# Softmax reciprocals as powers on GpSimd, two products of zeros at the start, and a new instruction order, in a kernel of two attention blocks

## Chip, cores, metric

One core of one Trainium2 chip. The metric is the device time of one launch in microseconds, the median of several runs; lower is better. A run is called slow when it is over 1.5% above the fastest of its kernel; verdicts use the other runs, called fast.

## The reference

Two independent attention blocks over x of 2048 x 640, 32 heads of width 20, in bf16. The outputs are laid side by side. Condensed, with masks, heads and shapes as in the reference:

```python
# block A: sliding window of 256
scores = jnp.einsum("bhqd,bhkd->bhqk", q, k) * (Dh ** -0.5)
mask = (idx[:, None] - idx[None, :] >= 0) & (idx[:, None] - idx[None, :] < 256)
p = softmax(jnp.where(mask, scores, -1e9)); a = (p @ v) @ wo
# block B: linear attention, phi(t) = where(t > 0, t + 1, exp(t)) + 1e-6
num = phi(q) @ (phi(k).T @ v); den = phi(q) @ phi(k).sum(0) + 1e-6
b = (num / den) @ wo
```

## The kernel before

The kernel builds a graph of small operations and then emits them in one list, ORDER, that a search outside the kernel wrote. An entry names an operation and the engine that does it: P is TensorE (PE), A ScalarE (ACT), D VectorE (DVE), G GpSimd (POOL), S SyncE (SP). SP only issues transfers; GpSimd issues many of them too. **Each engine works through its entries in exactly that order.** An entry that isn't ready holds back everything behind it on its engine.

The end of one of 16 groups of block A (a group is four heads and half of the 2048 rows): the value products leave numerators and denominators in PSUM. They are copied to ON, of which there are two. Four of ON's rows are the denominators. One transfer (den1) gathers them in RC, in a compact shape of 128 x 32, where they are inverted into RD. A second one (den2) writes the reciprocals to DRAM, and a third (den3, in four parts) spreads them over the rows of RB, of which there is one. Only then can DVE multiply the numerators by them (norm).

```python
def evac(e, rg=rg):
    copy(e, ON[nb][:, rg * NX : (rg + 1) * NX], FB[box[rg]][:])
# ... nb alternates between 0 and 1 from group to group
dma(QS, lambda q: q.dma_start(out=RC[nb][:], in_=ON[nb][Dh : Dh + 97 : 32, :]), ...)           # den1
pl.op({"DVE": 0.34}, lambda e: nc.vector.reciprocal(out=RD[nb][:], in_=RC[nb][:]), ...)         # recip
dma(QS, lambda q: q.dma_start(out=DR[nb][:]..., in_=RD[nb][:]), ...)                            # den2
for j in range(4):                                                                              # den3
    dma(QS, lambda q, j=j: q.dma_start(out=RB[32 * j : 32 * j + 32, :], in_=DR[nb][j : j + 1, :].to_broadcast([32, TQ])), ...)
pl.op({"DVE": 1.22}, lambda e: nc.vector.tensor_tensor(out=dst, in0=ON[nb][:], in1=RB[:], op=ALU.mult), ...)  # norm
```

The number in a `pl.op` is what the search takes for the operation's duration. At the start, PE runs seven products of zeros, then turns four blocks of x by products with a unit matrix, and then makes V as soon as WV is there.

```python
for _ in range(7):
    nc.tensor.matmul(FB[0], lhsT=E1[0][:, 0:P], rhs=E1[0][:, 0:NX], start=True, stop=True)
```

The softmax here doesn't subtract the row's maximum and nothing guards it: scores larger than these inputs give would overflow.

## Time and profile before

| | before |
|---|---|
| median time, us | 265.92 (3 runs), 267.27 with the run made beside the changed kernel |
| span of the profiled run, us | 263.8 |
| busy: PE / ACT / DVE / GpSimd, us | 247.4 / 210.1 / 171.4 / 68.6 |
| PE at half clock after the start, us | 6.8 in two stretches |

The prediction below shows the lines and reads them.

### The profile page before, as it was taken

To read this page: it belongs to the slowest core of one execution; us is meant where nothing else is said; L and a number is where in the kernel's file an instruction comes from. 1 tells how busy PE (TensorE), PEld (TensorE's weight loads), DVE (VectorE), ACT (ScalarE), POOL (GpSimd) and SP (SyncE) were. 2 spreads that over 40 slices of the span, in tenths; PEclk is the share of its full clock that TensorE was granted. 3 is DMA by queue.
4 is the path that set the end of the run, shared out by engine and by line. 5 is a ranking of instruction groups with operands and counts; after the bars stand their busy time and mean duration, and the time that the engine had idled before them with its cause. 6 is when DMAs were issued, how large, how long until landed. Compare 5 with 4: busy or idle time off the path is not lost.

```text
span 263.8 us, 10316 instructions
## 1 busy us (share of the span) xinstructions
PE 247.4 (94%) x4407; PEld 146.0 (55%) x4439; DVE 171.4 (65%) x388; ACT 210.1 (80%) x236; POOL 68.6 (26%) x156
## 2 busy tenths in 40 slices
PE   6899999999879999999999999987898999999994
PEld 2555555565545545545666666544555555577772
DVE  1226476698958675755362634988999978775542
ACT  3648789899987998888868887999999999964213
POOL 8001010334411114242202156001313313264410
PEclk9799999999979999999999999999999999999999
DMA  7998953968938524394887968776688245253635
GB/s 202 257 114 208 235 119 115 148 160 120 178 102 148 140 68 126 70 180 93 246 177 184 323 195 150 132 211 138 153 194 231 57 133 190 98 165 111 236 134 197
DMA packets 68495, 42.46 MB, mean 161 GB/s; under 512 B 54858, under 2 KB 63306, under 8 KB 68438
## 3 DMA queue, kind: packets, MB, share of 16 engines
q1 hardware_dynamic: 61266, 32.48, 53.1%
q0 software_dynamic: 4560, 9.00, 13.5%
q8 instruction: 34, 0.56, 0.9%
q10 hardware_dynamic: 2624, 0.33, 0.8%
q14 instruction: 11, 0.09, 0.1%
HBM read 24.29 MB, written 10.59 MB: 132 GB/s over the span
## 4 chain that ended last, share of the span: by engine, by line
PE 74%; ACT 13%; issue 5%; DVE 5%; DMA 2%; SPq 0%; ACTq 0%
PE F L437 16%; PE F L470 9%; PE F L714 9%; PE F L758 9%; ACT PT L548 8%; PE U L542 8%; PE F L750 6%; PE F L648 6%; PE U L714 5%; PE F L835 3%; ACT E L741 3%; DMA WV<-in_A_wqkv_dram 2%; DVE R L743 1%; DVE ON L352 1%; DVE PT L577 1%
## 5 line engine op out<-in xcount | busy, mean ns | idle before, releaser
L548 ACT ACTIVATE PT<-U 128x2048 bf16<-128x2048 f32 x78 | 146.7, 1881 | 15.5 <-PE U L542 14.2
L577 DVE TENSOR_TENSOR PT<-PT,MK 128x512 bf16<-128x512 bf16 (+2 forms) x116 | 46.8, 426 | 18.1 <-ACT PT L548 18.1
L542 PE MATMUL U<-QK 20*64 20x128 bf16 (+4 forms) x1600 | 33.1, 252 | 3.3 <-ACT PT L548 2.9
L542 PEld LDWEIGHTS <-QK 20*64 20x64 bf16 x1600 | 15.4, 104 | 26.1 <-issue 24.7
L686 POOL DMA_DIRECT2D RB<-dr x35 | 17.7, 508 | 43.5 <-DMA dr<-RD 16.9
L750 PE MATMUL F<-W,X 128*128 128x320 bf16 x160 | 26.8, 303 | 1.8 <-DVE R L743 1.8
L741 ACT ACTIVATE E<-F 128x320 bf16<-128x320 f32 (+1 forms) x52 | 25.6, 502 | 3.5 <-PE F L750 3.1
L743 DVE SCALAR_TENSOR_TENSOR R<-F,E 128x320 bf16<-128x320 f32 (+1 forms) x47 | 25.9, 553 | 1.2
L458 POOL DMA_DIRECT2D dqk<-QK x29 | 15.3, 532 | 43.4 <-ACT WK L348 17.9
L835 PE MATMUL F<-X,WQ 128*128 128x512 bf16 x85 | 25.2, 383 | 1.1 <-issue 0.7
L758 PE MATMUL F<-R,XT 128*128 128x320 bf16 x160 | 25.9, 300 | 0.0
L470 PE MATMUL F<-WV,X 128*128 128x320 bf16 x120 | 23.1, 318 | 1.3 <-DMA WV<-in_A_wqkv_dram 1.3
L648 PEld LDWEIGHTS <-V 64*32 64x32 bf16 x1556 | 19.1, 93 | 8.6 <-issue 7.2
L648 PE MATMUL F<-PT,V 64*32 64x320 bf16 (+4 forms) x1452 | 23.6, 250 | 0.1
L352 DVE CAST QK<-F 128x512 bf16<-128x512 f32 x20 | 13.6, 690 | 13.8 <-PE F L437 13.7
L750 PEld LDWEIGHTS <-X 128*128 128x128 bf16 x160 | 15.1, 98 | 10.5 <-issue 3.5
L437 PE MATMUL F<-X,WK 128*128 128x512 bf16 x71 | 20.5, 380 | 0.3
L682 POOL DMA_DIRECT2D RC<-ON x11 | 8.1, 735 | 45.2 <-DVE E L742 15.5
L437 PE MATMUL F<-X,WQ 128*128 128x512 bf16 x67 | 19.4, 380 | 0.4
L352 DVE COPY ON<-F 128x512 f32<-128x512 f32 x22 | 14.7, 687 | 6.9 <-PE F L648 6.7
L758 PEld LDWEIGHTS <-XT 128*128 128x128 bf16 x160 | 14.8, 98 | 7.5 <-issue 1.0
L742 DVE TENSOR_SCALAR E<-E 128x320 bf16<-128x320 bf16 (+1 forms) x52 | 13.4, 258 | 6.9 <-ACT E L741 6.6
(104 smaller groups left out, 329.3 us busy)
## 6 DMA issues: line engine op xcount, KB each, us to landing
RB<-dr POOLq DMA_DIRECT2D x35, 128.0 KB, 3.8
RB<-dr SPq DMA_DIRECT2D x29, 128.0 KB
QK<-dqk SPq DMA_DIRECT2D x6, 512.0 KB
XT<-in_B_x_dram SPq DMA_DIRECT2D x5, 512.0 KB
out_dram<-WK SPq DMA_DIRECT2D x9, 160.0 KB
do<-OS SPq DMA_DIRECT2D x5, 256.0 KB
out_dram<-ST SPq DMA_DIRECT2D x6, 160.0 KB
out_dram<-ST POOLq DMA_DIRECT2D x6, 160.0 KB, 2.8
```

Of the source, the lines that this page charges most:

```text
L352: nc.vector.tensor_copy(out=dst, in_=src)
L437: mms.append((mm_t(NX), xread(slot, k) + [("wqk", i, m)], lambda ps, k=k: nc.tensor.matmul(ps[:], lhsT=WQK[i][:, k, m * P : (m + 1) * P], ...
L470: mms = [(mm_t(HALF), (xread(slot, k) if slot or kb > 3 else [("xb", kb)]) + [("wv", hf)], lambda ps, k=k, hf=hf: nc.tensor.matmul(ps[:, 0 ...
L542: nc.tensor.matmul(upper.at(1)[0][64 * rho : 64 * rho + 64, j, cc : cc + w], lhsT=QK[g][32 * j : 32 * j + Dh, kc : kc + 64], rhs=QK[g][32 ...
L548: nc.scalar.activation(out=pt, in_=upper.at(1)[0][:], func=ACT.Exp, scale=scale)
L577: nc.vector.tensor_tensor(out=p, in0=p, in1=mk, op=ALU.mult)
L648: nc.tensor.matmul(FB[box[rg]][32 * j : 32 * j + 32, qc : qc + w], lhsT=V[kb % NV][64 * rho : 64 * rho + 64, HV * h : HV * h + 32], rhs=PT ...
L714: mms = [(mm_t(HALF), [lkeys(c)] if not isinstance(lkeys(c), list) else lkeys(c), lambda ps, c=c, hf=hf: nc.tensor.matmul(ps[:, 0:HALF], l ...
L741: ({"ACT": act_ps(n)}, lambda e, ps: nc.scalar.activation(out=e1, in_=ps[:, 0:n], func=ACT.Exp), [], [("e1", i)]),
L750: mms = [(mm_t(HALF), [("x", slot, k), ("w1",)], lambda ps, k=k, b=b, hf=hf: nc.tensor.matmul(ps[:, 0:HALF], lhsT=X[slot][:, k, b * P : (b ...
L758: mms = [(mm_t(HALF), [("r1", tb), ("xt", c % 2)], lambda ps, tb=tb, c=c, hf=hf: nc.tensor.matmul(ps[:, 0:HALF], lhsT=XT[:, c % 2, tb, :], ...
L835: mms = [(mm_t(NX), [("x", slot, k)] + WQK0, lambda ps, k=k, c=c: nc.tensor.matmul(ps[:], lhsT=WQB[:, k, :].rearrange("p (f c) -> p c f", ...
```

## The change

The intent: take reciprocals off DVE, which is full in the ACT-bound stretches, by using GpSimd, which is idle for three quarters of the span; keep PE's clock up at the start; and let the search place everything anew. The diff, cut to what takes effect (a tile of mask constants and its products are also added, but the set that would use them is empty, and the unit matrix gets 64 more columns for them; ORDER's 150 lines of numbers are left out):

```diff
-    tinyo = T([P, 1], "tinyo", F32)
+    minus = T([P, 32], "minus", F32)
+    nc.vector.memset(minus[:], -1.0)
...
+                o.deps[0].deps += busy      # the first products of V wait for both products of zeros
...
+    def keep_busy(tb):
...
+        o = pl.op({"PE": mm_t(NX)}, lambda e: nc.tensor.matmul(FB[box[0]], lhsT=E1[0][:, 0:P], rhs=E1[0][:], start=True, stop=True), 1.0, (), (), after=[turns[tb]], ...)
...
-        pl.op({"DVE": 0.34}, lambda e: nc.vector.reciprocal(out=RD[nb][:], in_=RC[nb][:]), key, ...)
+        pl.op({"DVE": 0.34, "POOL": 0.3}, lambda e: nc.vector.reciprocal(out=RD[nb][:], in_=RC[nb][:]) if e == "DVE" else nc.gpsimd.tensor_tensor(out=RD[nb][:], in0=RC[nb][:], in1=minus[:], op=ALU.pow), key, ...)
...
+    for tb in (0, 2):
+        keep_busy(tb)
```

With the groups numbered 0 to 15, the new order gives GpSimd the reciprocals of groups 0, 4 to 9 and 11 to 14.

## The prediction

> **What bounds the kernel now.** I read the page of the kernel before first (busy shares, the 40 slices, the chain that ended last), then the busy times by stage, then the timeline and the 3.41 us windows around the two dips of the granted clock, then the waits.
>
> ```profile
> PE 247.4 (94%) x4407; PEld 146.0 (55%) x4439; DVE 171.4 (65%) x388; ACT 210.1 (80%) x236; POOL 68.6 (26%) x156
> ...
> PEclk9799999999979999999999999999999999999999
> ...
> PE 74%; ACT 13%; issue 5%; DVE 5%; DMA 2%; SPq 0%; ACTq 0%
> ```
>
> TensorE (PE) is busy 94% of the span and carries 74% of the chain. The clock row dips twice, in slices 2 and 12. The stages show that PE is not the bound everywhere (columns: stretch, its length, busy us and instructions by engine, clock, DMA share, GB/s):
>
> ```profile
> 0.00:55.00 55.00, 51.33 (x680) 28.00 (x689) 26.97 (x70) 40.28 (x53) 10.22 (x49) 0.97 0.84 172
> 55.00:78.00 23.00, 20.55 (x412) 12.09 (x419) 18.81 (x50) 21.87 (x28) 8.62 (x16) 0.95 0.81 149
> 78.00:168.00 90.00, 89.06 (x1707) 51.66 (x1701) 53.77 (x118) 75.18 (x69) 24.25 (x44) 0.99 0.69 160
> 168.00:231.00 63.00, 57.34 (x1303) 33.52 (x1316) 55.49 (x122) 61.26 (x63) 14.43 (x26) 1.00 0.58 153
> 231.00:264.00 33.00, 29.10 (x325) 20.76 (x323) 16.33 (x32) 11.50 (x27) 11.07 (x22) 0.99 0.50 169
> ```
>
> Three stretches belong to PE: 6 to 55 us, 78 to 168 us (89.06 of 90), and 231 us to the end. Two belong to ScalarE (ACT): 55 to 78 us (21.87 of 23) and 168 to 231 us (61.26 of 63), where a 1.88 us exponential starts about every 2.5 us and ACT's other work fills the rest. In those two stretches PE has slack. What PE loses at the start is this:
>
> ```profile
> 1.26 3.10 PE L312 MATMUL F<-E 128*128 128x512 bf16 x7 [1.26 <-DVE ones L308]
> 4.19 0.44 PE L487 MATMUL U<-ID,QK 128*128 128x128 bf16 x5
> 5.30 0.73 PE L487 MATMUL U<-ID,QK 128*128 128x128 bf16 x10 [0.66 <-DMA QK<-in_A_x_dram]
> 7.36 1.06 PE L470 MATMUL F<-WV,X 128*128 128x320 bf16 x4 [1.33 <-DMA WV<-in_A_wqkv_dram]
> ...
> 4.15:7.57 3.42, 1.43 (x18) 1.05 (x17) 1.15 (x3) 1.56 (x3) 2.21 (x7) 1.00 1.15 298
> 7.57:10.98 3.41, 3.41 (x18) 2.12 (x17) 0.20 (x1) 2.15 (x5) 0.00 (x0) 0.50 1.22 242
> 72.42:75.83 3.41, 1.77 (x79) 1.38 (x56) 2.35 (x6) 3.41 (x4) 0.79 (x2) 1.00 0.63 197
> 75.83:79.25 3.42, 3.42 (x64) 1.64 (x63) 1.81 (x6) 2.46 (x4) 0.00 (x0) 0.50 0.07 16
> 171.41:174.82 3.41, 2.52 (x77) 1.46 (x85) 2.72 (x6) 3.25 (x4) 0.00 (x0) 1.00 0.91 233
> ```
>
> PE waits 0.66 us for x and 1.33 us for WV. After each stretch of 3.41 us in which PE was busy only 1.43 or 1.77 us, the next 3.41 us run at half clock. A stretch with 2.52 us busy was not followed by one.
>
> **What the Trainium skill says.** "TensorE: Matmul & The Clock Gate", section "What's actually happening": a monitor gates the PE clock to half after an idle window and frees it after a busy one; the window is 3413 ns and free-running. The trace agrees: both dips last 3.41 us at 0.50. The page gives no share of activity that counts as idle; this trace brackets it between 1.77 and 2.52 us busy of 3.41. "GPSIMD Engine Reference", section 3.1, gives 4497 ns for a 2048-column fp32 add of two tensors; its 32-column share is about 70 ns beside a fixed cost. It has nothing on a power, and no GpSimd instruction of the kernel before has two tensor inputs. The small selects there take 0.24 to 0.53 us, so I take 0.3 to 1.5 us for one power, an estimate. "SBUF — State Buffer", section "Who interferes with whom": a VectorE (DVE) instruction with two SBUF inputs and a GpSimd (POOL) instruction that reads SBUF block each other. The mask multiplications (116, mean 426 ns) are of that kind, so a power may be held for some tenths of a us. The trace before cannot show it.
>
> **The change part by part.**
>
> 1. *Powers on GpSimd.* The order gives GpSimd 11 of the 16 reciprocals. DVE loses 11 x 0.348 us (row L683) = 3.8 us. DVE also waited for the denominators to land before three of the 16, 2.5 us in all (row L683 of the waits), but none of that shows as a leading part of the chain. By itself I give this 0.2 us.
>
> 2. *Copies moved.* Counting both orders, ACT loses four Q/K copies (0.586 each), one turn of x (0.69), one weight shuffle (0.91), a G, a z and an ON copy (0.42, 0.43, 0.59), and gains one output copy (0.43): -5.0 us of 210. DVE gains the same at its own rates: 4 x 0.69 + 0.82 + 0.50 + 0.485 + 0.49 + 0.69 - 0.49 = 5.3 us, less the 3.8 us: +1.4 us of 171. So ACT room is bought with DVE room, and the reciprocals pay for most of it.
>
> 3. *Where that lands.* I summed each engine's work between the same score units in both orders, with the durations of the profile's rows (PE: 0.136 us per 320 columns, 0.216 per 512, as the chain shows). Up to score unit 12 (about 55 us): PE 43.7 before, 44.1 after. Units 12 to 20 (to 78 us): ACT 23.3 and 23.3, DVE 20.1 and 19.6. Units 20 to 52 (to 168 us): PE 80.1 and 80.3, ACT 78.5 and 75.8, but PE is the bound there, so ACT's 2.7 us are worth nothing. Units 52 to 77 (to 231 us): ACT 65.7 and 65.0, PE 49.5 and 50.3. After unit 77: PE 29.1 and 28.7. Only the last two pay: -0.6 us (0.7 scaled by 210 busy over 222 summed) in the ACT stretch, and -0.4 us of PE work pulled out of the tail into that stretch's slack. The +0.2 us in units 20 to 52 goes against them. Sum: -0.8 us.
>
> 4. *The two products of zeros.* They add 2 x 0.216 us of PE work, in time where PE waits for a DMA, so they delay nothing while the data is late. They lift the busy time of the idle window from 1.43 to about 1.9 us. That is inside the bracket of 1.77 to 2.52, so the chance that the clock holds is some 60%. If it holds, 3.41 us at half clock become full: a gain of 1.7 us, in a PE-bound stretch, so it is passed on. The window is free-running, so not every execution of the kernel before need pay it. Expected: -0.9 us.
>
> 5. *The start's DMA order.* WV's first half is now issued second instead of fourth on SP, but three blocks of x now come behind it. The first V product stands behind the second zeros, which stand behind the third turn, so it needs the same 880 KB as before (three blocks of 160 KB and 400 KB of WV). The second half of WV is issued before the other weights instead of at 7.16 us. Two value projections in a row can then run, and the fourth turn no longer divides them at half clock. I give it -0.3 us.
>
> 6. *The hole at 73 to 75 us.* PE waits 0.60 us for an exponential and 1.04 us for DVE's R, and the half clock at 75.83 follows (another 1.7 us). The new order has the same load there and shuffles the B products between units 18 and 22 differently. I take an even chance that the dip goes or a similar one stays, and a small chance of a new one elsewhere: -0.5 us.
>
> Sum: -0.2 - 0.8 - 0.9 - 0.3 - 0.5 = -2.7 us. I set +0.2 us against it for longer chains of the denominators. 265.9 - 2.5 = **263.4 us**.
>
> **The rivals.**
>
> *The clock dips anyway.* For it: 1.9 us busy is nearer 1.77, which dipped, than 2.52, and the turns now wait longer for x, since WV is ahead of it. Against: with the window placed otherwise, the first V products fall into it. It leaves the time at about 264.8 us.
>
> *GpSimd's power is slow, and the normalisations wait.* Each chain is: denominators out, power, two DMAs (3.8 us for the broadcast, section of DMA issues), then a 1.2 us product in DVE's fixed order. The new order leaves some 3 to 5 us from broadcast to product, so a power of up to about 1.5 us is hidden; of 3 us or more, up to 11 products would stall DVE by 1 to 2 us each, half of it in the ACT-bound stretch where DVE is 88% busy. It would make the time 265 to 269 us. Against it: GpSimd is idle 74% of the span.
>
> *The new order removes both dips and fits better everywhere.* The two dips (3.4 us) with the holes at 6 and 73 us (about 3 us) and the 1 us of part 3 make 7 us: 258.5 to 260 us. Against it: the work per stage hardly moves, and holes tend to come back elsewhere.
>
> **Range and chances.** The first and third rivals set the lower half, the second and a new hole the upper. 80% range: 260.4 to 266.8 us. Faster by over 2% means below 260.6 us, which asks for nearly all of the third rival: 0.12. Slower by over 2% means above 271.2 us, past even the slow-power rival: 0.03. Within 2%: 0.85.
>
> **What the profile after would show.** The clock row has no dip in the second slice, and the stretch from about 4 to 7.5 us has 1.9 us or more of PE busy. GpSimd has 11 powers of 0.3 to 1.5 us, and DVE 5 reciprocals. ACT's busy time falls by about 5 us, DVE's rises by about 1. The exponentials from unit 52 on still start every 2.5 us. The tail after the last exponential is 33 us, less 0.4. It would be wrong if DVE shows waits of some us for the broadcast denominators (RB), if the first dip stays, or if the B products make a new hole of over 1.5 us between 55 and 78 us.

## The result

| | before | changed |
|---|---|---|
| median, us | 267.27 (4 runs, 265.11 to 269.84) | 290.56 (4 runs, 288.32 to 292.56) |
| ratio of fast runs | 1 | 1.0899 (95%: 1.0754 to 1.1043) |
| span of the profiled run, us | 263.8 | 287.8 |
| busy: PE / ACT / DVE / GpSimd, us | 247.4 / 210.1 / 171.4 / 68.6 | 257.5 / 206.3 / 173.0 / 126.9 |
| PE at half clock after the start, us | 6.8 | 20.5 |

A ratio is the mean time of one kernel's fast runs over that of the kernel before in the same rounds, so it isn't quite the ratio of the medians. The change is slower by 9%. From the changed kernel's page: the busy line, the clock in 40 slices, and the group of the new GpSimd instruction (count, busy us and mean ns, then idle time before it); last, the group of the reciprocals on DVE in the kernel before.

```profile
PE 257.5 (89%) x4441; PEld 147.8 (51%) x4441; DVE 173.0 (60%) x387; ACT 206.3 (72%) x227; POOL 126.9 (44%) x163
...
PEclk9999999998999999977999997799998899999999
...
L722 POOL TENSOR_TENSOR RD<-RC,minus 128x32 f32<-128x32 f32 x11 | 60.8, 5530 | 36.7 <-DMA RC<-ON 31.7
...
L683 DVE RECIPROCAL RD<-RC 128x32 f32<-128x32 f32 x16 | 5.6, 348 | 2.6 <-DMA RC<-ON 2.5
```

**One power takes 5.5 us**, where the search had 0.3 and I had 0.3 to 1.5 (mean 5.53, median 5.46). PE's busy share fell by five points, and the clock dips in four places, none of which was there before. (PE's busy time rose although only two products were added: at half clock the same products take longer: below, ten take 2.87 us in a4 and 1.52 in a1.) The stages of the changed kernel:

```profile
0.00:55.00 55.00, 52.84 (x699) 28.61 (x700) 31.56 (x80) 39.50 (x49) 18.24 (x56) 1.00 0.79 163
55.00:78.00 23.00, 18.29 (x356) 10.77 (x355) 15.70 (x43) 18.44 (x24) 7.96 (x15) 0.93 0.74 149
78.00:168.00 90.00, 82.87 (x1488) 46.39 (x1487) 48.33 (x102) 65.99 (x59) 42.28 (x35) 0.96 0.59 146
168.00:231.00 63.00, 54.99 (x1142) 30.19 (x1144) 46.95 (x105) 50.41 (x48) 32.93 (x30) 0.92 0.63 138
```

Nothing is wrong in the first 55 us: PE even does more there than before (52.84 us against 51.33). From then on neither PE nor ACT fills its stage. In the waits (who <- what it waited for: us in total, times, longest), DVE's long stand for RB, the spread reciprocals, is new. The last line is from the kernel before, where it was 1.7 us in one place.

```profile
DVE OS L732 <- DMA RB<-dr: 18.1, 5, 7.9
...
DVE QK L732 <- DMA RB<-dr: 8.4, 2, 5.4
...
DVE QK L693 <- DMA RB<-dr: 1.7, 1, 1.7
```

And in the list of SP's own waits:

```profile
SPq L723 <- POOL RD L722: 26.8, 6, 7.0
```

SP stood 27 us at transfers that wait for a power, and loads for other stages stand behind those. The largest hole shows how it goes (timeline of the changed kernel: a line of GpSimd, two of DVE and one of PE, then the 3.41 us windows of the clock):

```profile
114.47 5.46 POOL L722 TENSOR_TENSOR RD<-RC,minus 128x32 f32<-128x32 f32 x1 [4.93 <-DMA W<-in_A_wo_dram]
...
127.29 1.23 DVE L732 TENSOR_TENSOR OS<-ON,RB 128x1024 bf16<-128x1024 f32 x1 [7.85 <-DMA RB<-dr]
...
128.63 0.69 DVE L361 CAST QK<-F 128x512 bf16<-128x512 f32 x1
...
129.37 1.49 PE L480 MATMUL F<-WV,X 128*128 128x320 bf16 x5 [6.24 <-DVE QK L361]
...
122.19:125.60 3.41, 0.94 (x6) 0.39 (x4) 0.00 (x0) 2.21 (x3) 2.04 (x4) 1.00 0.51 167
125.60:129.01 3.41, 0.00 (x0) 0.00 (x0) 1.72 (x3) 0.00 (x0) 0.00 (x0) 0.50 1.00 155
129.01:132.43 3.42, 3.06 (x34) 1.43 (x34) 1.94 (x6) 0.87 (x1) 2.55 (x1) 0.50 0.50 146
```

The power ends at 119.9 us, the reciprocals are spread by 127.3, and DVE has stood still for 7.85 us. The copy that frees PE's bank (at 128.63) is behind the product in DVE's order, so PE stands still for 6.24 us. That makes a nearly idle window, and the clock is at half for the next 6.8 us.

### The profile page after: what moved, and what is told of

It is laid out like the page before. It is cut to its first block, busy times and chain, and to the rows that moved or that the text cites. A ratio compares the mean times of both kernels' runs of the same rounds, so it can differ in the third digit from the quotient of the medians.

```text
span 287.8 us, 10335 instructions
## 1 busy us (share of the span) xinstructions
PE 257.5 (89%) x4441; PEld 147.8 (51%) x4441; DVE 173.0 (60%) x387; ACT 206.3 (72%) x227; POOL 126.9 (44%) x163
## 3 DMA queue, kind: packets, MB, share of 16 engines
q0 software_dynamic: 4416, 8.87, 11.8%
## 5 line engine op out<-in xcount | busy, mean ns | idle before, releaser
L722 POOL TENSOR_TENSOR RD<-RC,minus 128x32 f32<-128x32 f32 x11 | 60.8, 5530 | 36.7 <-DMA RC<-ON 31.7
L780 ACT ACTIVATE E<-F 128x320 bf16<-128x320 f32 (+1 forms) x52 | 25.6, 501 | 11.8 <-PE F L874 5.7
L468 POOL DMA_DIRECT2D dqk<-QK x35 | 18.4, 530 | 35.4 <-DVE QK L361 19.1
L789 PE MATMUL F<-W,X 128*128 128x320 bf16 x160 | 28.9, 311 | 3.5 <-DVE R L782 3.1
L570 PEld LDWEIGHTS <-QK 20*64 20x64 bf16 x1600 | 16.3, 105 | 27.8 <-issue 26.4
L874 PE MATMUL F<-X,WQ 128*128 128x512 bf16 x100 | 29.5, 393 | 0.0
L480 PE MATMUL F<-WV,X 128*128 128x320 bf16 x120 | 19.9, 306 | 6.2 <-DVE QK L361 6.2
L725 POOL DMA_DIRECT2D RB<-dr x27 | 13.7, 509 | 25.6 <-DVE V L361 7.7
L361 DVE CAST QK<-F 128x512 bf16<-128x512 f32 x24 | 16.3, 688 | 13.6 <-PE F L447 12.6
L753 PE MATMUL F<-WV,R 128*128 128x320 bf16 x90 | 18.0, 313 | 5.5 <-DVE XT L782 2.6
L447 PE MATMUL F<-X,WQ 128*128 128x512 bf16 x75 | 20.5, 380 | 0.0
L753 PE MATMUL F<-W,OT 128*128 128x320 bf16 x80 | 16.9, 325 | 3.8 <-DMA RB<-dr 2.3
L361 DVE CAST G<-F 128x320 bf16<-128x320 f32 (+2 forms) x21 | 10.2, 487 | 15.8 <-PE F L853 6.9
```

What stands on the lines that cost most here:

```text
L361: nc.vector.tensor_copy(out=dst, in_=src)
L447: mms.append((mm_t(NX), xread(slot, k) + [("wqk", i, m)], lambda ps, k=k: nc.tensor.matmul(ps[:], lhsT=WQK[i][:, k, m * P : (m + 1) * P], ...
L570: nc.tensor.matmul(upper.at(1)[0][64 * rho : 64 * rho + 64, j, cc : cc + w], lhsT=QK[g][32 * j : 32 * j + Dh, kc : kc + 64], rhs=QK[g][32 ...
L722: pl.op({"DVE": 0.34, "POOL": 0.3}, lambda e: nc.vector.reciprocal(out=RD[nb][:], in_=RC[nb][:]) if e == "DVE" else nc.gpsimd.tensor_tenso ...
L753: mms = [(mm_t(HALF), [lkeys(c)] if not isinstance(lkeys(c), list) else lkeys(c), lambda ps, c=c, hf=hf: nc.tensor.matmul(ps[:, 0:HALF], l ...
L780: ({"ACT": act_ps(n)}, lambda e, ps: nc.scalar.activation(out=e1, in_=ps[:, 0:n], func=ACT.Exp), [], [("e1", i)]),
```

## The experiments

**Theory, slow power:** the power's 5.5 us lengthen a chain whose slack the order had used up. **Rivals:** the new order packs worse by itself; GpSimd's queue, held for 5.5 us, starts other transfers late. In all of them, "(wrong)" marks a kernel whose result is wrong on purpose. "Measured" gives the median of all runs of a kernel, slow ones too.

| run | what it is | ratio of fast runs to before (95%) |
|---|---|---|
| changed | 11 powers | 1.090 (1.075 to 1.104) |
| a1 | all reciprocals on DVE | 0.995 (0.989 to 1.001) |
| a2 | product in place of the power (wrong) | 0.994 (0.988 to 1.000) |
| a3 | old order, 11 powers | 1.116 (1.110 to 1.123) |
| a4 | a1 without the zeros | 0.997 (0.991 to 1.003) |
| b2 | power on 8 of 32 columns (wrong) | 0.991 (0.982 to 0.999) |
| b3 | power on 16 columns (wrong) | 1.012 (1.001 to 1.023) |
| b4 | queue held, mostly not the chain (wrong) | 1.044 (1.037 to 1.052) |
| d1 | queue held, never the chain (wrong) | 0.995 (0.987 to 1.003) |
| d2 / d3 | powers in the first 5 / last 6 groups | 1.042 (1.034 to 1.049) / 1.041 (1.033 to 1.049) |
| b1 / e1 | later products, with power / product (e1 wrong) | 1.083 (1.075 to 1.091) / 1.023 (1.009 to 1.038) |
| c2 / c3 | chain's transfers on GpSimd, power / product (c3 wrong) | 1.089 (1.079 to 1.099) / 0.995 (0.987 to 1.003) |
| c1 / e2 | both moves, power / product (e2 wrong) | 1.077 (1.070 to 1.084) / 1.030 (1.009 to 1.050) |
| c4 | a1 again, five rounds | 0.995 (0.988 to 1.001) |

### a1: the same order, no power

```diff
-lambda e: nc.vector.reciprocal(...) if e == "DVE" else nc.gpsimd.tensor_tensor(..., op=ALU.pow)
+lambda e: nc.vector.reciprocal(...)
```

> The changed kernel with its new order and its zeros, but all 16 reciprocals on DVE, each at the place where the order has it. Theory 'slow power' (one power on GpSimd takes 5.5 us, and the broadcast denominators come too late for DVE's fixed order): 262 to 267 us, no DVE wait for RB of several us, no hole of over 3 us on PE. Rival 'worse order' (the new order itself packs worse): 280 to 290 us, the holes at 61, 123, 175, 219 and 250 us stay.

Measured: 263.52 us (before, same rounds, 265.46). The clock and stages of a1:

```profile
PEclk9999999999999999999999999999999999999999
...
78.00:168.00 90.00, 89.91 (x1710) 51.95 (x1716) 57.35 (x125) 73.02 (x65) 20.79 (x39) 1.00 0.69 167
168.00:231.00 63.00, 58.89 (x1289) 33.67 (x1281) 55.68 (x123) 60.10 (x58) 12.86 (x24) 1.00 0.57 148
```

PE fills its stage from 78 to 168 us again, and no dip is left. The new order isn't worse; the power is the whole loss.

### a2: the same engine and queue, a short instruction

```diff
-in1=minus[:], op=ALU.pow)
+in1=minus[:], op=ALU.mult)
```

> The changed kernel with the operation of the 11 GpSimd instructions set from power to product (a wrong result on purpose): same engine, operands, waits and order, only the duration of the instruction can differ. 'Slow power': GpSimd's instruction takes 0.2 to 0.6 us and the time is 261 to 267 us, within 1.5 us of the run with all on DVE. 'Reciprocals do not belong in GpSimd's queue' (they hold back the transfers that GpSimd issues behind them, whatever their length): 270 to 290 us. 'Worse order': 280 to 290 us.

Measured: 263.77 us. Its group of GpSimd instructions, with the mean of its one profiled run (a slow one; median 0.29 us, longest 1.22):

```profile
L722 POOL TENSOR_TENSOR RD<-RC,minus 128x32 f32<-128x32 f32 x11 | 4.2, 377 | 32.2 <-DMA RC<-ON 32.1
```

Same place, same operands, same waits, and only the duration differs. So it is not that a reciprocal stands in GpSimd's queue, but that it takes long.

### a3: powers in the old order

```diff
-pl.op({"DVE": 0.34}, lambda e: nc.vector.reciprocal(...), ...)
+pl.op({"DVE": 0.34}, lambda e, n=npv[0] - 1: nc.gpsimd.tensor_tensor(..., op=ALU.pow) if n in {0, 4, 5, 6, 7, 8, 9, 11, 12, 13, 14} else nc.vector.reciprocal(...), ...)
```

> The kernel before in its old order, with the reciprocals of the same 11 groups as powers on GpSimd. 'Slow power': each of 11 chains is 5.1 us longer and the old order has 3 to 6 us of slack from broadcast to product, so 275 to 290 us. 'Worse order': 265 to 268 us, as before.

Measured: 296.07 us, above my range. The old order loses even more: the loss doesn't need the new order.

### a4: without the zeros

```diff
-lambda e: nc.tensor.matmul(FB[box[0]], lhsT=E1[0][:, 0:P], rhs=E1[0][:], start=True, stop=True), 1.0
+lambda e: None, 1.0
```

> The run with all reciprocals on DVE, without the two products of zeros. If the zeros keep the clock up at the start: a half-clock stretch of 3.4 us near 7 to 11 us comes back in most executions and the time is 1 to 2 us longer than with them. If they do nothing: the same within 0.7 us.

Measured: 264.04 us; 0.997 against a1's 0.995, with overlapping intervals. **Inconclusive.** The two profiles do differ at the start. First a1's, then a4's first value products:

```profile
7.42 1.52 PE L480 MATMUL F<-WV,X 128*128 128x320 bf16 x10
```

```profile
7.04 2.87 PE L480 MATMUL F<-WV,X 128*128 128x320 bf16 x10
```

Ten products take 1.52 us with the zeros and 2.87 us without, that is at half pace. But in a2, which has the zeros, half pace also lasted until 10.3 us, so one profile of each doesn't settle it.

The other profiled runs add to this. Of the 16 with the zeros, eleven make the first ten value products at full pace, and five (a2, b3, b4, d2, e1) at half. Of the three without (before, a3, a4), one (a3) is at full pace. In d2 the first dip is back in spite of the zeros, after a window with 1.18 us of PE busy time:

```profile
4.08:7.49 3.41, 1.18 (x12) 0.60 (x10) 0.00 (x0) 1.44 (x3) 2.36 (x8) 1.00 1.17 312
7.49:10.90 3.41, 3.40 (x16) 2.04 (x17) 0.82 (x1) 0.74 (x2) 0.00 (x0) 0.50 1.36 228
```

In the new order, the seventh exponential starts at 35.5 to 35.8 us in the runs at full pace and at 37.0 to 38.0 in the others. So the zeros do not ensure full pace. Whether they make it more frequent is open.

### b2 and b3: a shorter power

```diff
+nc.gpsimd.tensor_tensor(out=RD[nb][:, 0:8], in0=RC[nb][:, 0:8], in1=minus[:, 0:8], op=ALU.pow)    # b3: 16
+nc.gpsimd.tensor_tensor(out=RD[nb][:, 8:32], in0=RC[nb][:, 8:32], in1=minus[:, 8:32], op=ALU.mult)
```

> The changed kernel with the power over 8 of the 32 columns and a product over the other 24 (a wrong result on purpose). If the power costs by the column: about 1.4 us for 8 columns, the chain is about 1.4 us longer than was planned for, and the time is 263 to 267 us, as the prediction's statement that a power of up to 1.5 us is hidden. If its cost is fixed: 5 us and 285 to 292 us.

> The same with 16 columns by power and 16 by product (a wrong result on purpose). By the column: about 2.8 us, and 266 to 274 us, since the prediction put the slack at 3 to 5 us from broadcast to product with landings of 3.5 to 3.8 us in it. If the loss grows in proportion from zero, a power of 2.8 us gives half of the 26 us: 276 us.

Measured: 267.16 us and 274.55 us (each just above its range), on a chip where the kernel before took 268.85. Two of b3's four runs are slow; its ratio is that of the other two, 273.79 and 271.05 us, and its verdict is unclear. The groups of b2, 8 columns by power and 24 by product:

```profile
L722 POOL TENSOR_TENSOR RD<-RC,minus 128x8 f32<-128x8 f32 x11 | 20.4, 1858 | 30.4 <-DMA RC<-ON 30.4
...
L722 POOL TENSOR_TENSOR RD<-RC,minus 128x24 f32<-128x24 f32 x11 | 3.2, 291 | 0.0
```

Most powers took about 1.67 us for 8 columns, 3.0 for 16 and 5.46 for 32: 0.16 us for a column and 0.4 us besides. The loss over a1 (0.995) is none, 1.7 and 9.5 points. It doesn't grow in proportion: 3 us are mostly hidden, 5.5 are not. That fits a slack of a few us.

### b4 and d1: GpSimd held, the chain not

```diff
+nc.gpsimd.tensor_tensor(out=RD[nb][:], in0=RC[nb][:], in1=minus[:], op=ALU.mult)
+nc.gpsimd.tensor_tensor(out=SCR[:], in0=RC[nb][:], in1=minus[:], op=ALU.pow)      # read by nobody
# d1 besides: in ORDER, 24 transfers of these 11 chains from G to S
```

> The changed kernel where a short product (0.3 us) makes what the denominators' chain reads (a wrong result on purpose) and the same power follows on GpSimd, into a tile that nobody reads: GpSimd's queue is held for 5.5 us as in the changed kernel, but the power isn't in the chain where the next transfer is issued by SP (6 of the 11); where GpSimd issues it (5 of the 11) it still is. 'Chain alone': 270 to 278 us. 'GpSimd's held queue alone' (its other transfers start late): 287 to 292 us, as the changed kernel. If neither part of it matters: 263 to 266 us.

> As the run with only the queue held (a short product makes what the chain reads, the power follows into a tile that nobody reads; a wrong result on purpose), and the 24 transfers of those 11 chains that GpSimd issued are issued by SP. GpSimd is held for 5.5 us eleven times, and no step of the denominators' chain stands behind it. 'The chain is all that matters': 263 to 268 us. 'The held queue costs by itself' (relay writes and stores that stand behind it): 274 to 282 us, as the run with only the queue held (1.044).

Measured: b4 281.36 us (1.044), between its two ranges; d1 265.18 us (0.995), as 'the chain is all that matters' had it. In d1 the powers are all there:

```profile
L723 POOL TENSOR_TENSOR SCR<-RC,minus 128x32 f32<-128x32 f32 x11 | 61.3, 5573 | 0.0
```

Sixty-one us of powers on GpSimd cost nothing that shows, as soon as no step of these 11 chains stands behind them. b4's loss came from the chains' own transfers that GpSimd had still to issue after the power. The held queue as a cause of its own is out, and so is a slow-down of other engines by the power itself.

### d2 and d3: which stage

```diff
-lambda e: nc.vector.reciprocal(...) if e == "DVE" else nc.gpsimd.tensor_tensor(..., op=ALU.pow)
+lambda e, n=npv[0] - 1: nc.gpsimd.tensor_tensor(..., op=ALU.pow) if n in {0, 4, 5, 6, 7} else nc.vector.reciprocal(...)   # d3: {8, 9, 11, 12, 13, 14}
```

> The changed kernel with powers in the first five of the 11 groups (47 to 149 us, mostly where PE is the bound), DVE reciprocals in the other six. If every long chain costs alike: 5 of 11, 274 to 277 us. If a delay counts only where PE is the bound: nearly the whole loss, 280 to 290 us. If it counts only where ACT is the bound: 264 to 268 us.

> The changed kernel with powers in the last six of the 11 groups (164 to 256 us, where ACT is the bound, and after it). If every long chain costs alike: 6 of 11, 276 to 279 us. The losses of this run and of the one with the first five, each over the run with all on DVE, add up to the changed kernel's 25 us, if the chains don't act on each other.

Measured: 277.17 and 277.19 us (before: 267.21). Over a1 that is 4.7 and 4.6 points, together 9.3 of the changed kernel's 9.5. **The losses add up**, and long chains cost where PE is the bound and where ACT is: in d3's profile, 10.9 of the 13.4 us that it falls behind a1 come between the 51st and the 77th of the 78 exponentials, where ACT is the bound in the kernel before, and 0.1 us after the last.

### b1, c2, c1 and their controls e1, c3, e2: can the wait be moved away?

b1: in ORDER, the product of each of the 11 groups moved later, by 0.7 to 4.2 us of PE work, and with six of them the store of the result. c2: 31 transfers behind the powers moved from SP to GpSimd. c1: both. The controls have the short product in place of the power.

```diff
# b1, ORDER: the entry of "norm" of 11 groups (and of six stores) stands later; the kernel's code is the same
# c2, ORDER: e.g.
-200:S
+200:G
# e1, c3, e2 besides
-op=ALU.pow
+op=ALU.mult
```

> The changed kernel with its powers, but the DVE product that needs the broadcast denominators stands later in DVE's order for the 11 groups with a power: as far as its dependents let it, by 0.7 to 4.2 us of PE work (for six of them by 3.6 us or more). 'DVE's fixed order' (the loss is DVE standing at the product while copies behind it would free PE's banks): DVE's wait for RB falls from 26.5 us to under 15 and the time to 270 to 282 us. 'Longer chain as such' (the time is lost wherever the product stands, through the buffers that it frees and the output that needs it): 286 to 292 us.

> The changed kernel with its powers, only the 31 transfers moved from SP to GpSimd; the products stay where they were on DVE. 'Fixed queues': between the changed kernel and the run with both freed, 272 to 286 us, since DVE still stands at the products. 'Longer chain as such': 286 to 292 us.

> The changed kernel with its 5.5 us powers, the later products of the run before, and the transfers behind each of the 11 powers (31 that SP issued) issued by GpSimd itself. In the run with later products DVE no longer waited for RB, but SP still stood 24 us at transfers that wait for a power, with loads queued behind them (PE then waited 6.5 us for XT). 'Fixed queues' (a 5.5 us power costs what stands in order behind it, on DVE and on SP): with both freed, 266 to 276 us, SP's wait for the power gone. 'Longer chain as such' (buffers and late outputs): still 284 to 292 us.

> Control for the later products: the same edited order with the short product in place of the power (a wrong result on purpose). If moving the DVE products costs nothing by itself: 263 to 267 us, and the run with later products (291) says that freeing DVE gives nothing back. If the move costs (buffers come free later): 270 to 280 us, and that run says less.

> Control for the two: the same 31 transfers on GpSimd, with the short product in place of the power (a wrong result on purpose). If moving the transfers costs little by itself: 263 to 267 us. If GpSimd's issue (about 0.5 us each, in order) is a load of its own: 267 to 275 us, to be taken off the other two.

> Control for later products with the transfers on GpSimd: the same order and engines with the short product in place of the power (a wrong result on purpose). Free of cost: 263 to 268 us. If the two moves cost: 270 to 280 us, and then most of that run's 1.077 is the price of the moves.

Measured: b1 291.44, c2 293.09, c1 287.1 us; the controls e1 270.94, c3 265.9, e2 271.92. b1 and c1 lie where 'longer chain as such' had them, c2 above both of its ranges (two of its four runs are slow). In b1, DVE's stand is mostly gone (0.7 and 3.1 us, from 18.1 and 8.4), and the time is nearly the same. From b1's waits (DVE's, SP's own, PE's):

```profile
DVE OS L732 <- DMA RB<-dr: 0.7, 1, 0.7
...
SPq L723 <- POOL RD L722: 24.1, 6, 7.0
...
PE F L797 <- DMA XT<-in_B_x_dram: 6.5, 1, 6.5
```

PE now stands 6.5 us for a load that was queued on SP behind a transfer that waits for a power. In c1, SP's wait for the power is gone too, but DVE stands elsewhere, and what PE needs is behind that in DVE's order (timeline of c1):

```profile
127.01 1.23 DVE L732 TENSOR_TENSOR OS<-ON,RB 128x1024 bf16<-128x1024 f32 x1 [4.84 <-DMA RB<-dr]
128.15 0.42 DVE L616 TENSOR_TENSOR PT<-PT,MK 128x512 bf16<-128x512 bf16 x1
128.62 0.62 PE L687 MATMUL F<-PT,V 64*32 64x256 bf16 x40 [4.26 <-DVE PT L616]
...
195.14 0.35 DVE L722 RECIPROCAL RD<-RC 128x32 f32<-128x32 f32 x1 [4.75 <-DMA RC<-ON]
195.41 0.43 DVE L361 CAST G<-F 120x320 bf16<-120x320 f32 x1
195.89 1.26 PE L687 MATMUL F<-PT,V 64*32 64x256 bf16 x60 [3.73 <-DVE G L361]
```

Each of the two waits of PE ends 0.05 us after the DVE instruction that the trace names. The first of these stood behind a product that waited 4.84 us for RB, the second behind a reciprocal whose denominators had not landed.

The controls say what the moves cost: the transfers nothing (c3, 0.995), the later products 2.8 points (e1 over a1). So b1's powers cost 5.9 points over e1, and c1's 4.8 over e2, against 9.5. Later products hide about two fifths to a half of the power's loss, and cost about a third of it back; the controls' intervals, 1.5 to 2 points either way, leave that rough. **My first theory of the way the loss travels, DVE's fixed order at the products alone, fell**: SP's queue (b1) and other instructions in DVE's order (c1) are also places where a late chain can be felt, and freeing one shows the next.

### c4: does the rest of the change pay?

The same kernel as a1.

> The new order and zeros with all reciprocals on DVE once more, in five rounds, to see whether it beats the kernel before: the three rounds gave 0.995 (0.989 to 1.001). The head is about 2 us earlier in its profile and both half-clock stretches are gone, so 0.988 to 0.998; 1.000 or more if that was chance.

Measured: 264.47 us (before 267.38), 0.995 (0.988 to 1.001). Three and five rounds agree on half a per cent, and neither interval excludes a ratio of 1. It is the best correct version found, by a margin that isn't clear of noise.

### The account of the slack

This table is from the traces of a1 and of the changed kernel: the time from the end of a group's reciprocal or power to the start of its product on DVE, in us. In between lie the two transfers.

| group | 0 | 4 | 5 | 6 | 7 | 8 | 9 | 11 | 12 | 13 | 14 |
|---|---|---|---|---|---|---|---|---|---|---|---|
| a1 | 9.7 | 11.0 | 8.7 | 9.9 | 13.1 | 12.6 | 13.6 | 11.8 | 10.5 | 9.0 | 8.4 |
| changed | 8.6 | 7.3 | 7.4 | 7.4 | 8.2 | 11.1 | 12.7 | 10.7 | 8.3 | 7.0 | 7.2 |

In the changed kernel five groups stand at 7.0 to 7.4 us, which is what the two transfers take. Take 7.2 us as the floor. Then a1 has a slack of 1.2 to 6.4 us, 3.6 on average. A power takes 5.1 us more than a reciprocal on DVE (5.46 against 0.34), so the shortage, summed over groups that lack slack, is 19.6 us: 10.0 in the first five, 9.6 in the last six. For b3 (2.9 us more) it is 4.8 us, for b2 (1.6 us more) 0.5 us. These are estimates from the traces. Measured over a1, at 267 us: 25 us, 12.4 and 12.3 us for the halves, 4.5 us for b3, none for b2. The sums come near, but two things speak against taking the account as it stands. First, the floor isn't fixed. In a1 the products of groups 5, 6 and 14 already waited about 1 us each for RB, though they started 8.4 to 9.9 us after the reciprocal:

```profile
DVE OS L732 <- DMA RB<-dr: 2.0, 2, 1.1
...
DVE QK L732 <- DMA RB<-dr: 1.0, 1, 1.0
```

By that sign they had no slack before the product, and with 5.1 us for each of them the shortage would be 25.0 us. Second, the parts do not fit. Where the changed kernel falls behind a1 can be read from the starts of the 78 exponentials in the two traces:

| exponentials | 13 to 17 | 17 to 29 | 29 to 37 | 37 to 51 | 51 to 53 | 53 to 67 | 67 to 69 | 69 to the end |
|---|---|---|---|---|---|---|---|---|
| groups with a power whose product falls there | 0 | | 4, 5 | 6, 7 | 8 | 9 | 11 | 12, 13, 14 |
| falls behind a1, us | 4.5 | -0.1 | 7.3 | 1.6 | 4.7 | 0.4 | 3.9 | 4.5 |
| shortage by the account, us | 2.6 | | 4.9 | 2.5 | 0 | 0 | 0.5 | 9.1 |

The account has nothing for group 8 and twice what is lost for the last three, so its equal halves are partly luck. That a short delay is hidden and a longer one is not is what b2, b3 and the changed kernel show together; how much slack each group has is not shown.

The clock is part of it. Stretches at half clock after the start were 0 us in a1, 3.4 in b2, 6.8 in b3, 10.2 in b4 and 20.5 in the changed kernel. The changed kernel's idle gaps of PE of over 0.15 us sum to 25.4 us, a1's to 7.2 (each with the 1.3 us before the first product). The gaps are 18.3 us more. In the 20.5 us at half clock PE was busy for 15.6, and by estimate half of that, 7.8 us, is lost. That makes 26.1, against 26.4 us between the spans. What a hole alone would cost, without the half clock after it, was not tested.

## Why the prediction was wrong, point by point

- **The step that failed is the one that sized the power**: "so I take 0.3 to 1.5 us for one power, an estimate". It was worked out from a page's sum of two tensors and from selects in the trace, neither of which is a power. A product of the same shape did take 0.29 us (a2); a power took 5.46. With it fell part 1 of the sum (-0.2 us), the "+0.2 us for longer chains", which became +25, and the chance of 0.03 for slower by over 2%, which stood for a time "past even the slow-power rival".
- **The second rival had the right mechanism and the wrong size.** It said that a power of 3 us or more would stall DVE by 1 to 2 us in each of up to 11 groups. In the trace DVE stood 26.5 us in all, in seven of the 16 products, up to 7.9 us in one. But the rival made only 265 to 269 us of it, as if most of a stall on DVE were hidden where ACT is the bound. d3 shows the opposite: the last six groups cost as much as the first five, most of it in that stretch. It left out SP's queue (26.8 us at transfers that wait for a power) and that a hole in PE's work halves the clock afterwards. And its "some 3 to 5 us from broadcast to product" did not hold for groups 5, 6 and 14, whose products in a1 waited for RB even without a power. Its claim that a power of up to about 1.5 us is hidden held (b2: power and product together about 1.9 us, no loss).
- **Without the power the number was right, for reasons that held in part.** I said 263.4 us; a1 took 263.52 and c4 264.47. That the first agrees to 0.1 us is luck: against the kernel before of their rounds the gain was 0.5%, 1.3 to 1.5 us and not clear of noise, where I had 2.5. ACT's busy time fell by 4.0 us (I had 5.0). DVE's rose by 1.6 in the changed kernel (1.4). The two dips of the profile before are gone in a1 and a4.
- **The zeros** (-0.9 us) are not decided. The dip in the second slice did go in a1, but in a4 without the zeros too, where half pace from the start lasted until 10.2 us instead; and in d2, with the zeros, the dip was there. Nor is there one limit inside the bracket of 1.77 to 2.52 us: in a3 a window with 1.78 us of PE busy time was followed by full clock, in c1 one with 1.94 us by half (places in the last section).
- **The start's order and the hole at 73 us.** The first V product started at 7.4 us in a1, as before, and the seventh exponential at 35.8 us instead of 37.8. The hole came back (1.1 us at 70.8 us), but no dip followed.
- **Powers held by DVE.** "SBUF — State Buffer", section "Who interferes with whom", on which I rested that a power may be held for some tenths of a us, has DVE instructions of two SBUF inputs and GpSimd reads block each other. A few GpSimd instructions were longer by some tenths up to 1 us (a2: 1.22 against 0.29; powers: 6.05 against 5.46), which fits, but no run isolates it; d1 shows no cost of it.

## What to carry to other kernels

Before an operation is moved to an idle engine, time that very operation there, in that shape; another operation of the same engine and form says nothing (0.29 us for a product, 5.46 us for a power). In a kernel whose orders are fixed on every engine, a chain off the critical path has a slack that can be read from the trace, as time between an input's earliest arrival and its use; a delay within it is free (b2: 1.6 us more in each of 11 chains, no loss), and beyond it it can reach the end through whichever queue is next (5.1 us more: 25 us), though here not by the group that such an account names. An engine that is idle three quarters of the time can be held for 61 us at no cost that shows (d1), as long as nothing in that chain stands behind it.

## What the Trainium skill lacked or had wrong

- "GPSIMD Engine Reference", section 3.1 and the table of engine selection (4.1), give GpSimd as about two times slower than DVE for elementwise work of two inputs, and no duration of a power. Here a power of 128 x 32 in fp32 took 5.46 us, against 0.29 us for a product on GpSimd and 0.35 us for DVE's reciprocal, so about 16 times DVE's time for the same result; 0.16 us per column and about 0.4 us besides.
- "TensorE: Matmul & The Clock Gate", section "What's actually happening", gives the window (3413 ns; every dip here lasts one to three of them, 3.41 to 10.24 us) and no share of activity. Nor do the traces give a sharp one (PE's busy time is partly modelled, and some traces lack a few products). The lowest PE busy time of a window that was followed by half clock was 0 (a3), the highest 1.94 us (c1, from 176.93 us). A window with 1.78 us was followed by full clock (a3, from 77.48 us). A window at half clock with 2.46 us was followed by more of it (changed kernel, from 176.80 us).
- No page that I used says that the profile's clock column can show 1.00 at the start where PE goes at half pace: in a4, ten value products took 2.87 us there, and 1.52 us in a1. a4's trace has no clock record before 10.24 us.
